# The first two terms of three output products taken into the last score steps, and the last denominators inverted as 16 columns, in a fused attention and MLP block

## The chip, the core and the metric

The kernel runs on one core of a Trainium2 chip. The metric is the device time of one execution in microseconds, lower is better. A core has TensorE (matmuls), VectorE, ScalarE and GpSimd, which run their own instruction queues and wait for each other by semaphores, and DMA queues that are fed here by SyncE. Results of matmuls land in PSUM, which has eight banks of 128 partitions x 512 fp32 values.

## The reference

One transformer block with a modulated layernorm ahead of each half. S = 2048 rows, D = 512, 32 heads of 16 columns, F = 1792, fp32.

```python
x = A_x
mod = (_silu(c) @ w_mod).reshape(c.shape[0], 6, 1, -1)
sa, ca, ga, sb, cb, gb = (mod[:, 0], mod[:, 1], mod[:, 2], mod[:, 3], mod[:, 4], mod[:, 5])
h = _layernorm(x, axis=-1) * (1 + ca) + sa
x = x + ga * _A_ref(h, A_wqkv, A_wo)
h = _layernorm(x, axis=-1) * (1 + cb) + sb
x = x + gb * _B_ref(h, B_w1, B_b1, B_w2)
return x
```

`_A_ref` is softmax attention over all rows, `softmax(q k^T * 16^-0.5) v`, followed by the output product with `wo`. `_B_ref` is `mish(h @ w1 + b1) @ w2`, with mish(a) = a * tanh(softplus(a)).

## The kernel before

**Precision.** A product of fp32 operands is made of three matmuls in the fast fp32 format: each operand is split into a high and a low part, and high x high, high x low and low x high are summed in PSUM. So one output product over D = 512 has four blocks k of 128 rows, with three terms each: 12 matmuls of 128 x 128 by 128 x 512.

**Steps.** Attention goes over 4 blocks of 512 queries (`qb`) and 8 groups of 4 heads (`g`); `n = 8 qb + g` counts the 32 pairs, and each has 16 steps, one for 128 keys. T = 512 steps in all. In a step the kernel emits:

- the scores of four heads for 128 keys, L531: matmuls whose contraction is 64 rows, so that each uses one half of the array's rows (a row group); ScalarE takes the exponential of each (L534);
- the maxima of the scores 20 steps ahead (L482, L484), as long as there is a later pair: `PRO` is 20, so the last 20 steps have no maxima;
- a part of the MLP of the query block before, taken from a queue of units (`units`, `next_part`). A unit of 12 matmuls is spread over two pairs of steps, six slots each. `mm_half` (L135) issues each slot twice, in the even step with the upper 64 rows of the contraction and in the odd one with the lower 64, both times in the row group that the step's own scores do not use;
- `pv` (L549), the product of probabilities and values for the step t - 2: eight passes, which use all rows.

In a step without maxima, f MLP halves stand in the list `beside` and the step's four scores in `mine`, spread between them. If f is under 4, o = (4 - f) // 2 of the scores move to the other row group. Halves of one bank in different row groups must not run at once, so the first half of a step waits for an exponential (`cur["after"]`), that of the score emitted behind the last half of the step before; `next_part` drops this wait when it starts a new unit.

**PSUM.** Six banks are a ring (`ring`, `NRING`) for scores, maxima and some tail products; two more have the tags `ms` (MLP units) and `acc` (probabilities times values). `free_banks` drops dependencies between ring instructions that touch different banks.

**End of a head group.** `evac` copies the 128 x 512 sums of a head group to `ot`; row 16 of each head's 32 rows holds the denominators. They are inverted by way of DMAs, and `od` times the inverse, split in high and low, becomes `o_hl`, the input of the output product (k = g // 2). For the very last group there is no time for DMAs: `evac_last` takes one matmul with a constant matrix `pick` (two passes, L610), which puts the head rows into partitions 64 to 127 and each head's denominator, 16 times, into partitions 0 to 63, and inverts those 64 x 512 values (L611).

**Tail.** After the last step `tail` computes the output product and the MLP of the last 512 rows, with nothing else to run beside. The output product is emitted as the terms k = 0, 1, 2 of four products of 128 rows (`wo_mms`, L1002), with `evac_last` after the first of them, and then k = 3 of all four, each followed by its addition to x (L1014) and a layernorm. Held-back MLP units of the query block before (`held`, L129) and the transposes (L1035) follow, and the last MLP. The weights `wos` and the first `w1s` are loaded at step T - 15 (`tail_loads`) into `ka` tiles that hold no keys any more (L970), the rows of x by the tail itself (L993).

All loads and stores are issued by SyncE from one queue, in the order of the hooks (`at`, `run_hooks`: two half-steps per step).

Of the kernel before, what the change touches and what calls it, by code (L numbers as in the profile page):

```python
# [8 lines left out]
F32 = mybir.dt.float32  # L9
# [9 lines left out]
def adaln_block(ctx: ExitStack, tc: tile.TileContext, x, wqkv, wo, w1, b1, w2, c, w_mod, out):  # L19
    nc = tc.nc  # L20
    P = 128
    S, D = x.shape[1], x.shape[2]
    F = w1.shape[1]
    H = 32
    DH = D // H
    DK = D // P
    FT = F // P
    TB = 512
# [4 lines left out]
    T = 16 * NIT  # L33
# [3 lines left out]
    VROW = NKC * 4 * VW + 16  # L37
    LEAD = 4
    PRO = 16 + LEAD
# [6 lines left out]
    x = x[0]  # L46
# [11 lines left out]
    woscr = dram.tile([DK, P, 2, D], F32, name="woscr")  # L58
# [4 lines left out]
    ident = cst.tile([P, P], F32, name="ident")  # L63
# [20 lines left out]
    gates = [cst.tile([P, D], F32, name=f"gate{i}") for i in range(2)]  # L84
# [61 lines left out]
    NRING = 6  # L146
    ring_t = ps.tile([P, NRING, TB], F32, name="ring")
    ring_at = [0]

    def ring(w=1):  # L150
        if w == 2 and ring_at[0] % 2:
            ring_at[0] += 1
        b = ring_at[0] % NRING
        ring_at[0] += w
        return ring_t[:, b, :] if w == 1 else ring_t[:, b:b + 2, :]
# [41 lines left out]
    def at(h, f):  # L197

        hooks.setdefault(h, []).append(f)
# [4 lines left out]
    ka = [kq.tile([P, S], F32R, name=f"ka{i}") for i in range(2)]  # L204
# [116 lines left out]
    with ExitStack() as es:  # L321
# [68 lines left out]
        for i in range(2):  # L390
            pr.append(ring())
            for k in range(DK):
                nc.tensor.matmul(pr[i][32 * k:32 * k + 32, :], sil[:, k:k + 1].to_broadcast([P, 32]), wma[i][:, k, :],
                                 start=True, stop=True)
# [34 lines left out]
        for tb in range(NB):  # L429
# [5 lines left out]
            for kind in (1, 0) if tb == 0 else (1,):  # L435
                fin = qk_unit(kind, 0, tb, "ring")
# [26 lines left out]
    ap = ctx.enter_context(tc.tile_pool(name="ap", bufs=1, reuse_waits="tile"))  # L463
# [90 lines left out]
    o_hl = {}  # L554
    st, mst = {}, {}
# [42 lines left out]
    def make_pick():  # L598
# [3 lines left out]
        for i, src in enumerate((cols[:, :, DH:DH + 1].to_broadcast([P, 4, DH]), cols[:, :, :DH])):  # L602
            nc.gpsimd.tensor_copy(pick[:, i, :].rearrange("p (h w) -> p h w", w=DH), src)

    def evac_last(dn):

        ot, od, rb = mst["last"]
        oh, ol = o_hl[NB - 1]
        r = slice(64, P)
        nc.tensor.matmul(dn, mst["pick"].rearrange("p a w -> p (a w)"), ot, start=True, stop=True)  # L610
        nc.vector.reciprocal(rb[r], dn[:64, :])  # L611
        nc.vector.tensor_mul(od[r], dn[r, :], rb[r])
        hi_copy("v", oh[r, DK - 1, :], od[r])
        lo_sub("v", ol[r, DK - 1, :], od[r], oh[r, DK - 1, :])

# [348 lines left out]
    last = NB - 1  # L964
    _, w1s, w2s, wos = state[last]

    def half_tile(t, j, scr):

        w = t[:, j * 2 * D:(j + 1) * 2 * D]
        nc.sync.dma_start(w.bitcast(F32), scr.rearrange("p v m -> p (v m)"))  # L970
        return w.rearrange("p (v m) -> p v m", v=2)

    def w1_tail(f):
        i, j = divmod(f % 8, 2)
        return load_w1(f) if i == 1 else half_tile(ka[(1, 0, 2, 3)[i]], j, w1scr[f])

    def tail_loads():
        for k in range(DK):
            wos[k] = half_tile(ka[(4, 0)[k // 2]], k % 2, woscr[k])
        for f in range(2):  # L980
            w1s[f] = w1_tail(f)

    def tail():

        oh, ol = o_hl[last]
        mp = mst["p"]
        y, xn = [], []
        for v in (y, xn):
            for i in range(4):
                v.append(ap.tile([P, D], F32, tag=f"p{i}", name="y", bufs=3 + i % 2))  # L990
        for i in range(4):
            r = 4 * last + i
            nc.sync.dma_start(y[i], x[r * P:(r + 1) * P, :])  # L993
        for f in range(4, 8):
            w1s[f] = w1_tail(f)
        accs4 = [bank("ms"), bank("acc")] + [None, None]

        def wo_mms(i, ks):
            s = slice(i * P, (i + 1) * P)
            seq = [(l, r, k) for l, r in ((oh, 0), (oh, 1), (ol, 0)) for k in ks]  # L1000
            for j, (l, r, k) in enumerate(seq):
                nc.tensor.matmul(accs4[i], l[:, k, s], wos[k][:, r, :], start=(k == 0 and j == 0),  # L1002
                                 stop=(k == 3 and j == 2))

        norms = []
        wo_mms(0, (0, 1, 2))
        evac_last(ring())
        wo_mms(1, (0, 1, 2))
        for i in (2, 3):
            accs4[i] = bank("ring")  # L1010
            wo_mms(i, (0, 1, 2))
        for i in range(4):
            wo_mms(i, (3,))
            nc.vector.tensor_add(y[i], accs4[i], y[i])  # L1014
# [73 lines left out]
        for u in range(FT + LAG):  # L1088
# [14 lines left out]
            f = u - LAG  # L1103
            if f >= 0:
                a_h, a_l = act.pop(f)
                w = w2s.pop(f)
                for i in range(4):
                    s = slice(i * P, (i + 1) * P)
                    for j, (l, r) in enumerate(((a_h, 0), (a_h, 1), (a_l, 0))):
                        nc.tensor.matmul(po[i // 2][:, i % 2, :], l[:, s], w[:, r, :], start=(f == 0 and j == 0),  # L1110
                                         stop=(f == FT - 1 and j == 2))
                    if f == FT - 1 and i % 2:
                        for q in (i - 1, i):
                            nc.vector.tensor_add(y[q], po[q // 2][:, q % 2, :], y[q])
                            r = 4 * last + q
# [9 lines left out]
    cur = {"left": [], "fin": None, "part": []}  # L1125
# [7 lines left out]
    def next_part(h):  # L1133

        if not cur["left"] and units and h >= units[0][0]():
            cur["fin"] = units.pop(0)[1]("ms")
            cur["left"] = list(pe_queue)
            cur.pop("after", None)
            pe_queue.clear()
        slots = []  # L1140
        for m in cur["left"]:
            if slots and len(slots[-1]) < 2 and m[0].shape[-1] <= TB // 2:
                slots[-1].append(m)
            else:
                slots.append([m])
        n = len(slots)
        k = n if n <= 8 else (n + 1) // 2
        cur["part"], cur["left"] = slots[:k], [m for l in slots[k:] for m in l]
# [24 lines left out]
    def step(t):  # L1173
        second = t % 2
        n, u = t // 16, t % 16 // 2
        tm = t + PRO
        run_hooks(2 * t)
        if t < 0:

            for i in range(2):  # L1180
                if tm < 16:
                    kb, jq = divmod(2 * tm + i, 8)
                else:
                    jq, kb = tm % 16 // 2, 2 * second + i
                max_pair(tm // 16, jq, kb)
            if second and tm % 16 == 15:
                neg_max(tm // 16)
            run_hooks(2 * t + 1)
            for f in ats.pop(t, []):
                f()  # L1190
            whole_units(2 * t + 1, CREDIT)
            do_specials(2 * t + 1)
            return
        s = 0 if second else 1
        own, others = ([score(n, j, v, 2 * u + i) for i in range(2) for j in range(2)] for v in (s, 1 - s))
        if not second and 1 < t < T:
            next_part(2 * t)
        part = list(cur["part"])
        f = len(part)
        if t >= T:  # L1200
            if t == T:
                cur["tag"] = "acc"
            run_hooks(2 * t + 1)
            pv(t - 2)
            whole_units(2 * t + 1, 8)
            do_specials(2 * t + 1)
            return
        if tm < T:
            o = max(0, (8 - f) // 2)
            mo, alone = maxima(tm // 16, tm % 16 // 2, s, o)  # L1210

            mine = [x for p in zip(mo, own) for x in p] + own[len(mo):]
        else:
            o = max(0, (4 - f) // 2)
            mine = own[o:] if second else own[:4 - o]
            alone = others[4 - o:] if second else others[:o]

            m = len(mine)
            if f > m:
                mine = [mine[(i * m) // f] if (i + 1) * m // f > i * m // f else None for i in range(f)]  # L1220
        beside = part + alone

        def emit(product):
            e = product()
            if e is not None and cur.pop("want", None):
                cur["after"] = e

        mid = False
        for i in range(max(len(mine), len(beside))):
            if i == len(mine) // 2:  # L1230
                run_hooks(2 * t + 1)

            if not f and tm < T and i == (2 if mst.get("norming") else 3):
                pv(t - 2)
                mid = True
            if i < f:
                last = i + 1 == f
                if i < len(mine) and mine[i] and not last:
                    emit(mine[i])
                for m in beside[i]:  # L1240
                    mm_half(m, second, cur.pop("after", None))
                if last:
                    cur["want"] = True
                    if i < len(mine):
                        emit(mine[i])
                    if second and not cur["left"]:
                        cur["fin"](2 * t + 2)
                        cur["fin"] = None
            else:
                for x in (*mine[i:i + 1], *beside[i:i + 1]):  # L1250
                    emit(x)
        if tm < T and tm % 16 == 15:
            neg_max(tm // 16)
        do_specials(2 * t + 1)
        if not mid:
            pv(t - 2)
        for f in ats.pop(t, []):
            f()
# [89 lines left out]
    for qb in range(NB - 1):  # L1348
        t0 = 32 * G * (qb + 1) + 16
        at(161, lambda qb=qb, t0=t0: block(qb, t0))  # L1350
    at(2 * T - 200, make_pick)
    at(2 * T - 30, tail_loads)
    for pp in range(2, NR):
        for b in (48, 112):
# [10 lines left out]
    t = T + 2  # L1365
# [32 lines left out]
```

## Time and profile before

| | |
|---|---|
| runs before (3) | median 1705.93 us, 1703.87 to 1709.53 |
| span of the profiled execution | 1705.4 us |
| TensorE busy | 1678.7 us, 98% |
| VectorE busy | 1439.9 us, 84% |
| ScalarE busy | 1364.9 us, 80% |
| GpSimd busy | 808.0 us, 47% |
| last L549 of the score stage begins | 1599.74 us |
| tail's first matmul | 1602.45 us |

The profile is one execution, and its span is measured from the first to the last instruction; a run's time is measured around it. In its rows a group stands as line, engine, operation, output<-inputs, tile sizes and a count; the timeline has start and duration in us ahead of it, and in brackets how long the engine had been idle and which instruction released it. PE is a matmul, PEld its weight load, DVE is VectorE, ACT ScalarE, POOL GpSimd, SPq SyncE's queue. The duration of a matmul is from its start until its result is in PSUM; matmuls are pipelined, and what one costs TensorE is the distance to the start of the next.

### The profile page before, as it was taken

How to read it: one execution, taken by the hardware profiler on the slowest of the kernel's cores; microseconds unless marked ns; L12 is line 12 of the kernel's file. 1: busy time of each engine (PE TensorE's matmuls, PEld its weight loads, DVE VectorE, ACT ScalarE, POOL GpSimd, SP SyncE). 2: the span in 40 equal slices, each digit the busy share in tenths (PEclk: the TensorE clock that was granted, in tenths of full speed). 3: DMA queues.
4: the chain of work that ended last, by engine and by line, in shares of the span. 5: the costliest groups of instructions: out<-in, count | busy, mean ns of one | idle time of the engine just before them, and what ended most of it. 6: DMA issues, size and time to landing. Idle time of an engine off the chain costs nothing.

```text
span 1705.4 us, 33628 instructions
## 1 busy us (share of the span) xinstructions
PE 1678.7 (98%) x12372; PEld 956.8 (56%) x12372; DVE 1439.9 (84%) x2368; ACT 1364.9 (80%) x2613; POOL 808.0 (47%) x829
## 2 busy tenths in 40 slices
PE   7999999999999999999999999999999999999999
PEld 5755655555445555555555555555555455554587
DVE  6888888888889998888889998888889988883377
ACT  6257777777778988888888988888888988888574
POOL 5155224665413464655423564555323655555442
PEclk9999999999999999999999999999999999999999
DMA  7677467777773342534355433424354433524261
GB/s 253 183 235 210 116 161 213 242 228 221 237 209 100 98 105 78 137 79 123 84 154 145 119 75 94 139 74 125 85 144 124 128 93 78 150 59 156 85 228 63
DMA packets 113997, 240.08 MB, mean 141 GB/s; under 512 B 24048, under 2 KB 49648, under 8 KB 107784
## 3 DMA queue, kind: packets, MB, share of 16 engines
q1 hardware_dynamic: 113832, 237.92, 48.8%
q8 instruction: 98, 1.61, 0.4%
q14 instruction: 67, 0.55, 0.1%
HBM read 179.95 MB, written 51.44 MB: 136 GB/s over the span
## 4 chain that ended last, share of the span: by engine, by line
PE 90%; DMA 4%; DVE 3%; ACT 1%; SPq 1%; issue 1%; POOL 0%; ACTq 0%; DVEq 0%; POOLq 0%
PE bk L549 28%; PE ring L482 21%; PE ring L531 19%; PE bk L135 12%; PE bk L129 3%; PE ring L1110 2%; PE ring L129 2%; DVE mx L484 1%; DMA qa<-mt 1%; DMA ka<-kscr 1%; DMA xt<-in_A_x 1%; PE ring L496 1%; ACT pr L534 1%; DMA w<-woscr 1%; DMA w<-w1scr 0%
## 5 line engine op out<-in xcount | busy, mean ns | idle before, releaser
L484 DVE TENSOR_REDUCE mx<-ring 128x1 f32<-128x512 f32 x1968 | 1222.1, 682 | 157.7 <-PE ring L482 134.1
L534 ACT ACTIVATE pr<-ring 128x512 f32<-128x512 f32 x2048 | 1085.6, 601 | 215.5 <-PE bk L135 131.2
L482 PE MATMUL ring<-ka,qa 64*128 64x512 f32 x1968 | 834.2, 427 | 5.2 <-DMA od<-ot 2.7
L531 PE MATMUL ring<-qa,ka 64*128 64x512 f32 x2048 | 724.5, 397 | 4.2 <-ACT pr L534 2.2
L482 PEld LDWEIGHTS ring<-ka,qa 64*128 64x128 f32 x1968 | 359.6, 184 | 405.8 <-DVE mx L484 341.2
L549 PE MATMUL bk<-pr,vg 128*32 128x512 f32 x4096 | 545.1, 604 | 0.0
L531 PEld LDWEIGHTS ring<-qa,ka 64*128 64x128 f32 x2048 | 373.8, 184 | 81.3 <-ACT pr L534 23.6
L135 PE MATMUL bk<-h,w 64*128 64x512 f32 (+1 forms) x1080 | 280.2, 393 | 0.1
L135 PE MATMUL bk<-w,a_h 64*128 64x512 f32 x632 | 213.0, 417 | 0.3 <-ACT pr L534 0.2
L135 PEld LDWEIGHTS bk<-h,w 64*128 64x128 f32 x1080 | 178.2, 184 | 12.3 <-ACT pr L534 3.7
L549 PEld LDWEIGHTS bk<-pr,vg 128*32 128x32 f32 x4096 | 80.7, 108 | 132.0 <-issue 124.6
L135 PE MATMUL bk<-w,a_l 64*128 64x512 f32 x316 | 124.0, 392 | 0.0
L135 PEld LDWEIGHTS bk<-w,a_h 64*128 64x128 f32 x632 | 104.7, 184 | 16.6 <-ACT pr L534 8.3
L899 POOL TENSOR_TENSOR y<-yd,y 128x512 f32<-128x512 f32 x44 | 56.8, 1292 | 89.5 <-ACT yd L898 84.4
L750 POOL TENSOR_TENSOR qq<-qq,rr 128x512 f32<-128x512 f32 x42 | 54.3, 1292 | 89.8 <-ACT rr L744 89.6
L734 POOL TENSOR_SCALAR qq<-ee 128x512 f32<-128x512 f32 x25 | 15.5, 619 | 168.0 <-ACT ee L728 168.0
L736 POOL TENSOR_TENSOR hb<-hb,ee 128x512 f32<-128x512 f32 x42 | 54.1, 1288 | 82.5 <-DVE ee L732 80.5
L135 PE MATMUL bk<-w,o_hl 64*128 64x512 f32 x288 | 79.6, 408 | 0.0
L98 POOL TENSOR_TENSOR a_l<-hb,a_h 128x512 fp32r<-128x512 f32 x53 | 72.0, 1359 | 4.4
L135 PEld LDWEIGHTS bk<-w,a_l 64*128 64x128 f32 x316 | 58.3, 184 | 3.9
L135 PE MATMUL bk<-h_h,wl 64*128 64x512 f32 x168 | 56.7, 418 | 0.0
L752 POOL TENSOR_TENSOR rr<-rr,qq 128x512 f32<-128x512 f32 x42 | 54.2, 1291 | 3.5
(189 smaller groups left out, 1844.2 us busy)
## 6 DMA issues: line engine op xcount, KB each, us to landing
ka<-kscr SPq DMA_DIRECT2D x124, 384.0 KB
w<-w2scr SPq DMA_DIRECT2D x56, 512.0 KB
w<-w1scr SPq DMA_DIRECT2D x46, 512.0 KB
vg<-vscr SPq DMA_DIRECT2D x32, 552.0 KB
qa<-qscr SPq DMA_DIRECT2D x124, 100.0 KB
kscr<-qh SPq DMA_DIRECT2D x16, 512.0 KB
qscr<-qh SPq DMA_DIRECT2D x32, 256.0 KB
hl<-in_B_w SPq DMA_DIRECT2D x28, 256.0 KB
```

What stands on the lines that cost most here:

```text
L98: (nc.gpsimd if eng == "p" else nc.vector).tensor_sub(lo, src, hi.bitcast(F32))
L129: nc.tensor.matmul(acc, l, r, start=start, stop=stop)
L135: i = nc.tensor.matmul(acc, l[64 * g:64 * g + 64], r[64 * g:64 * g + 64], start=start and not g, stop=bool(stop and g))
L482: nc.tensor.matmul(pm, qt[64 * s:64 * s + 64, qs * P:(qs + 1) * P], kt[64 * s:64 * s + 64, kb * TB:(kb + 1) * TB], start=True, stop=True)
L484: nc.vector.tensor_reduce(out=mxs[n][:, s, 4 * j + qs, kb:kb + 1], in_=pm, op=ALU.max, axis=AX.X)
L531: nc.tensor.matmul(p_, kt[64 * s:64 * s + 64, kc * P:(kc + 1) * P], qt[64 * s:64 * s + 64, :], start=True, stop=True)
L534: e = nc.scalar.activation(pr, p_, AF.Exp, scale=SCALE)
L549: nc.tensor.matmul(accs[n][32 * h:32 * h + 32, :], vgs[n][:, o:o + 32], pts.pop((t, h)), start=(kc == 0), stop=(kc == 15))
L736: (nc.vector if tail else nc.gpsimd).tensor_mul(hb, hb, ee)
L750: nc.gpsimd.tensor_mul(qq, qq, rr)
L752: nc.gpsimd.tensor_mul(rr, rr, qq)
L899: nc.gpsimd.tensor_add(y[i], yd, y[i])
```

## The change

Two edits. First, the terms k = 0 and 1 of the output products i = 0, 1, 2 of the last query block (6 of 12 matmuls each, 18 in all) are no longer emitted in the tail but, as halves, in the last 18 steps, in bank 5 of the ring, which the ring leaves out from step T - 20 until the tail; after each product VectorE adds it to the rows of x. For this the weights of k = 0, 1 and three blocks of x are loaded earlier. Second, the denominators of the last head group are gathered as 128 x 16 values by four matmuls with four columns of the identity, inverted, copied out to 16 equal columns each, and brought back to rows by four matmuls with the identity; the product with `pick` stays, for the head rows, which ScalarE copies to `od`.

```diff
+    kept = []
     def ring(w=1):
         if w == 2 and ring_at[0] % 2:
             ring_at[0] += 1
+        if kept and ring_at[0] % NRING == NRING - 1:
+            ring_at[0] += 1
...
+    def sums_last(cs):
+        ot = mst["last"][0]
+        for q in range(4):
+            nc.tensor.matmul(cs[:, 4 * q:4 * q + 4], ot[:, q * P:(q + 1) * P], ident[:, DH::32], start=True, stop=True)
+        rc = ap.tile([P, 16], F32, tag="rc", name="rc", bufs=2)
+        nc.vector.reciprocal(rc, cs[:, :16])
+        wide = ap.tile([P, TB], F32, tag="p0", name="wide", bufs=3)[:, :256].rearrange("p (q h d) -> p q h d", q=4, h=4)
+        mst["rc"] = wide
+        nc.vector.tensor_copy(wide, rc.rearrange("p (q h) -> p q h", h=4)[:, :, :, None].to_broadcast([P, 4, 4, DH]))
+
+    def heads_last(dn):
+        ot, od, _ = mst["last"]
+        nc.tensor.matmul(dn, mst["pick"].rearrange("p a w -> p (a w)"), ot, start=True, stop=True)
+        nc.scalar.copy(od[64:], dn[64:, :])
+
     def evac_last(dn):
-        ot, od, rb = mst["last"]
+        od, rc = mst["last"][1], mst["rc"]
         oh, ol = o_hl[NB - 1]
         r = slice(64, P)
-        nc.tensor.matmul(dn, mst["pick"].rearrange("p a w -> p (a w)"), ot, start=True, stop=True)
-        nc.vector.reciprocal(rb[r], dn[:64, :])
-        nc.vector.tensor_mul(od[r], dn[r, :], rb[r])
+        for q in range(4):
+            nc.tensor.matmul(dn[64:, q * P:(q + 1) * P], rc[:, q].rearrange("p h w -> p (h w)"), ident, start=True, stop=True)
+        nc.vector.tensor_mul(od[r], dn[r, :], od[r])
         hi_copy("v", oh[r, DK - 1, :], od[r])
         lo_sub("v", ol[r, DK - 1, :], od[r], oh[r, DK - 1, :])
...
+    FIRST = 3
+    first_of = {"left": [], "fin": None, "part": [], "next": 0}
+    ys = {}
+    def load_wos(ks):
+        for k in ks:
+            wos[k] = half_tile(ka[(4, 0)[k // 2]], k % 2, woscr[k])
+    def load_ys(js):
+        for i in js:
+            ys[i] = gates[i] if i < 2 else ap.tile([P, VROW], F32, tag="vg", name="vg", bufs=2)[:, :D]
+            r = 4 * last + i
+            nc.sync.dma_start(ys[i], x[r * P:(r + 1) * P, :])
     def tail_loads():
-        for k in range(DK):
-            wos[k] = half_tile(ka[(4, 0)[k // 2]], k % 2, woscr[k])
+        load_wos((2, 3))
         for f in range(2):
             w1s[f] = w1_tail(f)
+    def first_part(h):
+        u = first_of
+        if not u["left"] and u["next"] < FIRST:
+            i = u["next"]
+            u["next"] += 1
+            oh, ol = o_hl[last]
+            acc = ring_t[:, NRING - 1, :]
+            s = slice(i * P, (i + 1) * P)
+            seq = [(l[:, k, s], wos[k][:, v, :]) for l, v in ((oh, 0), (oh, 1), (ol, 0)) for k in range(2)]
+            u["left"] = [[(acc, l, r, j == 0, j == len(seq) - 1)] for j, (l, r) in enumerate(seq)]
+            u["fin"] = lambda: nc.vector.tensor_add(ys[i], acc, ys[i])
+        u["part"], u["left"] = u["left"][:2], u["left"][2:]
...
-                v.append(ap.tile([P, D], F32, tag=f"p{i}", name="y", bufs=3 + i % 2))
-        for i in range(4):
+                v.append(ys[i] if v is y and i < FIRST else ap.tile([P, D], F32, tag=f"p{i}", name="y", bufs=3 + i % 2))
+        for i in range(FIRST, 4):
...
-        wo_mms(0, (0, 1, 2))
+        kept.clear()
+        wo_mms(0, (2,))
+        sums_last(ring())
+        heads_last(ring())
         evac_last(ring())
-        wo_mms(1, (0, 1, 2))
+        wo_mms(1, (2,))
         for i in (2, 3):
             accs4[i] = bank("ring")
-            wo_mms(i, (0, 1, 2))
+            wo_mms(i, (2,) if i < FIRST else (0, 1, 2))
...
-            cur.pop("after", None)
+            if not first_of["left"]:
+                cur.pop("after", None)
...
         part = list(cur["part"])
+        if not second:
+            first_of["part"] = []
+            if t == T - PRO:
+                kept.append(NRING - 1)
+            elif T - PRO < t < T:
+                first_part(2 * t)
+        g = len(part)
+        part += first_of["part"]
         f = len(part)
...
-                    if second and not cur["left"]:
+                    if second and g and not cur["left"]:
                         cur["fin"](2 * t + 2)
                         cur["fin"] = None
+                    if second and first_of["part"] and not first_of["left"]:
+                        first_of["fin"]()
...
+    at(2 * (T - 29), lambda: load_wos((0, 1)))
+    at(2 * (T - 28), lambda: load_ys((0, 1)))
+    at(2 * (T - 12), lambda: load_ys((2,)))
     at(2 * T - 30, tail_loads)
```

## What is predicted

> **What bounds the kernel now.** I read the page first, for the engine that sets the time.
>
> ```profile
> span 1705.4 us, 33628 instructions
> PE 1678.7 (98%) x12372; PEld 956.8 (56%) x12372; DVE 1439.9 (84%) x2368; ACT 1364.9 (80%) x2613; POOL 808.0 (47%) x829
> PE 90%; DMA 4%; DVE 3%; ACT 1%; SPq 1%; issue 1%; POOL 0%; ACTq 0%; DVEq 0%; POOLq 0%
> ```
>
> TensorE is busy for 98% of the span and holds 90% of the chain that ended last. So the question is where matmul time is added and where it is taken away, and whether it is on that chain at both places. The change touches two places: the last steps of the score stage, and the first microseconds of the tail. I cut the span there. The 18 steps that will carry new matmuls (T-18 to T-1) run from the start of one probability-times-value group (L549, one per step) at 1551.96 to that of the 18th one after it, at 1599.74.
>
> ```profile
> core 0: us, PE busy (x) PEld busy (x) DVE busy (x) ACT busy (x) POOL busy (x), PEclk, DMA share, GB/s
> 1551.96:1599.74 47.78, 47.40 (x326) 21.69 (x325) 5.12 (x8) 42.28 (x83) 26.79 (x26) 1.00 0.26 95
> ...
> 1602.45:1611.78 9.33, 9.33 (x42) 7.26 (x39) 5.16 (x4) 0.59 (x1) 0.00 (x0) 1.00 0.96 335
> ```
>
> These 18 steps take 47.78 us, 2.654 us each. TensorE is busy for 47.40 of them, ScalarE for 42.28, and the granted clock is full. Two engines are near their limit, so the order inside one step decides. Here is one step from the timeline of TensorE, between two L549 groups; columns are start, duration, engine, line.
>
> ```profile
> 1589.17 1.07 PE L549 MATMUL bk<-pr,vg 128*32 128x512 f32 x8
> 1590.24 0.50 PE L135 MATMUL bk<-w,a_h 64*128 64x512 f32 x1
> 1590.24 0.49 PE L531 MATMUL ring<-qa,ka 64*128 64x512 f32 x1
> 1590.58 0.39 PE L135 MATMUL bk<-w,a_h 64*128 64x512 f32 x1
> 1590.58 0.39 PE L531 MATMUL ring<-qa,ka 64*128 64x512 f32 x1
> 1590.81 0.39 PE L135 MATMUL bk<-w,a_l 64*128 64x512 f32 x1
> 1590.82 0.39 PE L531 MATMUL ring<-qa,ka 64*128 64x512 f32 x1
> 1591.04 0.39 PE L135 MATMUL bk<-w,a_h 64*128 64x512 f32 x1
> 1591.04 0.39 PE L531 MATMUL ring<-qa,ka 64*128 64x512 f32 x1
> 1591.27 0.39 PE L135 MATMUL bk<-w,a_h 64*128 64x512 f32 x1
> 1591.51 0.40 PE L135 MATMUL bk<-w,a_l 64*128 64x512 f32 x1
> 1591.83 1.06 PE L549 MATMUL bk<-pr,vg 128*32 128x512 f32 x8
> ```
>
> A half of an MLP matmul (L135, 64 rows of the array) starts at the same moment as a score (L531, the other 64 rows): these two do run beside each other. But there are six halves and only four scores. After the fourth pair the halves go on alone, one every 0.23 us (1591.04, 1591.27, 1591.51), and L549, which needs all rows, waits for the last. A step is therefore six halves in a row (1590.24 to 1591.83, 1.59 us) and L549 (1.07 us): 2.66 us. The row group of the scores has two free places, that of the halves none. Two more rows: L135 alone over the 18 steps, and ScalarE in the step above.
>
> ```profile
> 1551.96:1599.74 47.78, 29.82 (x109) 18.55 (x108) 1.00 0.26 95
> ...
> 1590.78 2.06 ACT L534 ACTIVATE pr<-ring 128x512 f32<-128x512 f32 x4 [0.59 <-PE ring L531]
> ```
>
> The 108 weight loads of halves (second x) in 18 steps are six each: all steps are of this kind. The second row is ScalarE: four exponentials in 2.06 us, after 0.59 us of waiting for a score. In steps without other work ScalarE waits for TensorE, and not the other way round.
>
> **What the change adds to these steps.** Two rows of the chain of waits, in the tail, give the price of full matmuls and of transposes there.
>
> ```profile
> 1618.90 0.87 PE ring L1035 x8
> ...
> 1687.56 11.80 PE ring L1110 x51
> ```
>
> `first_part` appends two slots to the six, at every even step of the 18, and both steps of the pair issue them as halves: 9 x 2 x 2 = 36 halves. They are 18 matmuls of 512 columns (three products, two k, three terms). A half has 64 rows but the same 512 columns, and its place costs 0.23 us, as the step above shows; the 51 full matmuls in 11.80 us are 0.231 us each, the same. I calculate with 0.232.
>
> `mm_half` puts every half of a step into the row group that the step's own scores do not use. That is the group with no free place. So f goes from 6 to 8, and the step from 2.66 to 2.66 + 2 x 0.232 = 3.12 us. Over 18 steps 36 x 0.232 = 8.35 us. Waiting that is there now could cover some of it; but 18 x 2.66 = 47.9 us stand against 47.78 measured, so these steps hold hardly any, and I allow 0.15 us. I take **+8.2 us**. Bounds: nothing, if the halves found free places; and 18 x (0.34 + 0.232) = 10.3 us, if the change of bank between an MLP half and a new half cost the spacing of the step's first pair (1590.24 to 1590.58).
>
> The Trainium skill, TensorEngine Tiling (Array Packing), Overview, gives up to twice the speed for a contraction of 64 rows, because the tiles of the array work independently. The trace agrees only where the other row group has a matmul (the four pairs above); by that rule in full, 8 + 4 passes would fill six places and the steps would cost nothing, a rival below.
>
> **What else is added to the steps, at no cost.** The rows for it: a copy on VectorE in these steps, and DMA issues on SyncE.
>
> ```profile
> L898 DVE COPY yd<-bk 128x512 f32<-128x512 f32 x3 | 2.1, 692 | 16.2 <-PE bk L135 16.2
> ...
> 1553.95 3.21 SPq L970 DMA_DIRECT2D ka<-woscr  x4
> ...
> 1602.43 1.82 SPq L993 DMA_DIRECT2D y<-in_A_x  x4
> 1604.30 2.01 SPq L970 DMA_DIRECT2D ka<-w1scr  x4
> ```
>
> Three additions of a product into y on VectorE, 0.69 us each like the `yd` copy above, one every six steps; VectorE is busy for 5.12 of 47.78 us. An addition stands behind the unit's own last instruction in VectorE's queue, so the bank of the next unit is released first; the next new half comes over 1.5 us after the addition. If VectorE were full they would cost 2.1 us. The score ring loses one of six banks: a score then waits for the exponential of five scores back, at the latest the third of the step before, which is over by then. Two weight loads move from step T-15 to T-29, and three loads of x from the tail to T-28 and T-12.
>
> Issuing these five takes 2 x 0.8 + 3 x 0.45 = 3.0 us of SyncE's queue, against 47.78 us in which the DMA share is 0.26. They write a ka tile whose last pair ends before step T-32, the two gate tiles that only the weights' preparation read, and the v tile of the head group before the last, read up to T-15: none is still in use, so the queue is held for its 3.0 us at most, no matmul of the next step waits for what stands behind, and the tail's w1 loads go out 1.4 us earlier.
>
> **What the tail loses and gets.** The tail's first part is quoted with its rows, because TensorE has no gap in it, but a chain through VectorE runs beside.
>
> ```profile
> 1602.45 2.36 PE L1002 MATMUL bk<-ka,o_hl 128*128 128x512 f32 x9
> 1602.59 0.59 ACT L563 COPY ot<-bk 128x512 f32<-128x512 f32 x1 [1.77 <-PE bk L549]
> 1604.65 1.02 PE L610 MATMUL ring<-ot,pick 128*128 128x512 f32 x2
> 1605.71 3.35 DVE L611 RECIPROCAL rb<-ring 64x512 f32<-64x512 f32 x1 [5.10 <-PE ring L610]
> 1609.09 0.69 DVE L612 TENSOR_TENSOR od<-ring,rb 64x512 f32<-64x512 f32 x1
> 1609.82 0.42 DVE L93 CAST o_hl<-od 64x512 fp32r<-64x512 f32 x1
> 1610.28 0.69 DVE L98 TENSOR_TENSOR o_hl<-od,o_hl 64x512 fp32r<-64x512 f32 x1
> 1611.78 1.55 PE L1002 MATMUL bk<-ka,o_hl 128*128 128x512 f32 x6
> ```
>
> The 3.35 us reciprocal is over, with what follows, at 1610.97. TensorE comes to the matmuls that need it (k = 3) at 1611.78. So the reciprocal is hidden now, with 0.8 us to spare, and making it short gains nothing by itself. It is a condition of the other edit: with 18 matmuls fewer, TensorE would arrive 4.2 us earlier and wait.
>
> Two rows of the first 200 us have operations like those that are added.
>
> ```profile
> L399 PE MATMUL bk<-sel,row 128*128 128x1 f32 x16 | 1.9, 251 | 0.0
> L584 DVE RECIPROCAL rc<-sm 128x16 f32<-128x16 f32 x1 | 0.2, 240 | 0.0
> ```
>
> Removed: 18 x 0.232 = -4.18 us. Added: sums of four columns, 4 matmuls of two passes each (fp32 takes two, as L610 x2 for one matmul shows); the nearest row is the one-column matmuls at the start (L399). They take 1.9/16 = 0.119 us each although they stream one column: 8 x 0.119 = +0.95. The spreading back is 8 passes of 128 columns, like the transposes (L1035, 0.87 for 8): +0.87. The pick matmul stays (two passes). Waiting: `ot` is written until 1603.18, while three matmuls instead of nine cover only until about 1603.2; then a weight load that cannot be ahead of its matmul, and a change of tiling: +0.2. The 16-column reciprocal (0.24) and a copy of 256 columns (0.4 at most, by the cast of 512) run while the pick matmul does (0.86), so TensorE hardly waits for them. Then multiplication, cast and subtraction (0.69 + 0.42 + 0.69 and gaps, 1.9 us) run beside 15 matmuls (3.5 us). Sum: -4.18 + 0.95 + 0.87 + 0.2 = **-2.2 us**. Bounds: -3.9 if the small passes cost almost nothing, -0.3 if each cost as much as 512 columns (16 x 0.232 = 3.7).
>
> For the sums the Trainium skill, TensorE: Matmul & The Clock Gate, Back-to-back issue gap, counts about 60 cycles for any width from 1 to 64, 25 ns with its floor; an estimate from that page is 0.2 us for 8 passes and a gain of 2.9 in the tail. The measured 0.119 us decides here.
>
> Behind 1611.78 nothing is changed: additions, layernorm, transposes and the MLP follow in the same order, and TensorE stays the bound, so the gain goes through to the end.
>
> **Sum.** 1705.4 + 8.2 - 2.2 = 1711.4 us of span. The median of the runs shown, 1705.93, is 0.5 above the profiled span, so I predict 1711.9 for the median, +0.35%.
>
> **The rivals.**
> *Free places are used (not slower).* The two halves stream in the two places that the scores leave free. The step stays at 2.66, and only the tail's gain is left: 1711.9 - 8.2 = 1703.7. Against it: the free places are in the other row group, and the trace shows halves starting alone at 0.23 us. It decides if the step stays below 2.8 us. 8%.
> *The exponentials become the chain (more slower).* The first half of a step waits for the exponential of the score that was issued after the last half. That score now comes after the eighth. From the step's start: 0.34 + 6 x 0.232 = 1.73, then 0.54 to the exponential (1590.24 to 1590.78) and 0.6 for it: 2.87, below 3.12. But ScalarE has eight MLP operations in these steps, two in each of four rows, of which three stand here.
>
> ```profile
> L534 ACT ACTIVATE pr<-ring 128x512 f32<-128x512 f32 x74 | 38.3, 604 | 5.4 <-PE ring L531 5.0
> L741 ACT ACTIVATE rr<-ee,two 128x512 f32<-128x512 f32 x2 | 1.5, 746 | 0.0
> L725 ACT ACTIVATE ee<-hb,hcap 128x512 f32<-128x512 f32 x2 | 1.5, 744 | 0.0
> ...
> L744 ACT ACTIVATE rr<-rr 128x512 f32<-128x512 f32 x2 | 1.3, 658 | 0.0
> ```
>
> Where one falls between the third and the fourth, the step is 2.87 + 0.74 = 3.61, 0.5 more: with six such steps +3, 1714.9. Against it: they now fall behind the fourth. 9%.
> *The tail gives nothing back.* If the sums, the short reciprocal, the copy and the second pass follow each other with their waits exposed, some 2 us of idle TensorE take the place of what was removed: 1711.9 + 2.2 = 1714.1. For it: four crossings between engines; against it: the pick matmul covers them. 10%.
> *My forecast*: 70%, from 1709.8 (tail at -3.9 and some cover) to 1713.5. The remaining 3% are causes not listed.
>
> **How the numbers follow.** A measurement of this kernel tells a change from none at about 0.3%, 5.1 us, so slower begins at 1711.05. The forecast lies above it, with some four fifths of its chance; with the two slower rivals this gives 0.70 x 0.83 + 0.09 + 0.10 = 0.77 for slower. The rest of the forecast and the first rival are within 0.3%: 0.70 x 0.17 + 0.08 = 0.20. Faster would need the first rival and another 3 us: 0.03. The range 1709.0 to 1714.9 holds the forecast and the two slower rivals, and leaves out the first.
>
> **What would show it.** Right: the timeline shows eight halves in a step and L549 groups 3.05 to 3.15 us apart, 18 steps in about 56 us; the tail's k = 3 matmuls start some 9.3 - 2.2 = 7.1 us after the first tail matmul; the stretch behind has its length unchanged. Wrong: steps below 2.9 us (free places), idle TensorE released by L534 at the steps' starts (exponentials), or idle TensorE between the pick matmul and the second pass (tail). If the steps come out at 2.66, the prediction is wrong in its largest term.

## The result and the profile after

| | before | after |
|---|---|---|
| runs | median 1706.74 us (22 runs, 1702.20 to 1711.67) | median 1711.82 us (22 runs, 1708.49 to 1717.95) |
| ratio to before | | 1.0027, 95% interval 1.0019 to 1.0035 |
| span of the profiled execution | 1705.4 us | 1709.6 us |

The change makes the kernel slower by 0.27%, some 4.6 us by the ratio; the two medians lie 5.1 us apart. That the predicted 1711.9 came within 0.1 us of the median is luck: the predicted difference (+6.0) was 0.9 us larger than that of the medians, and with more runs the median of before moved up by 0.8 us. The page of the changed kernel:

```profile
span 1709.6 us, 33702 instructions
PE 1685.0 (99%) x12406; PEld 961.5 (56%) x12406; DVE 1438.6 (84%) x2372; ACT 1367.6 (80%) x2614; POOL 808.2 (47%) x829
PE 94%; DVE 2%; DMA 2%; ACT 1%; issue 0%; POOL 0%; SPq 0%; ACTq 0%; DVEq 0%; POOLq 0%
```

TensorE got 6.3 us more to do and its share of the chain rose. Busy time by stretch shows where (column 2 is the length, the rest as in the prediction's first view of this kind); the cuts are the same events as in the kernel before: 18 steps, last L553 group (L549 before), tail to the first k = 3 matmul, k = 3, rest.

```profile
1551.07:1605.90 54.83, 54.83 (x361) 28.23 (x361) 6.70 (x11) 44.64 (x83) 26.82 (x26) 1.00 0.20 69
1605.90:1608.61 2.71, 2.71 (x25) 0.68 (x24) 1.00 (x2) 0.72 (x2) 1.27 (x1) 1.00 0.03 13
1608.61:1615.71 7.10, 7.10 (x39) 5.27 (x36) 2.36 (x5) 1.17 (x2) 0.00 (x0) 1.00 0.96 359
1615.71:1618.51 2.80, 2.80 (x14) 2.27 (x13) 1.59 (x4) 0.00 (x0) 0.00 (x0) 1.00 0.06 20
1618.51:1709.60 91.09, 87.09 (x408) 71.89 (x406) 71.33 (x97) 53.98 (x82) 34.70 (x38) 1.00 0.37 136
```

The stretches of the kernel before that were not shown yet:

```profile
1599.74:1602.45 2.71, 2.71 (x25) 0.68 (x25) 0.69 (x1) 1.07 (x3) 1.28 (x1) 1.00 0.00 0
...
1611.78:1614.56 2.78, 2.78 (x13) 2.26 (x12) 1.76 (x4) 0.00 (x0) 0.10 (x1) 1.00 0.27 109
1614.56:1705.40 90.84, 86.87 (x407) 71.70 (x405) 71.27 (x97) 53.95 (x82) 34.60 (x38) 0.99 0.36 136
```

The 18 steps went from 47.78 to 54.83 (+7.05), the tail up to k = 3 from 9.33 to 7.10 (-2.23), everything between and behind by 0.0, 0.0 and +0.25. The sum of the two places is +4.8 us, 0.28% of the time, which is the measured ratio. The stretch ahead of the 18 steps was 0.89 us shorter in this execution; the same point came anywhere from 1549.78 to 1555.62 us in the executions shown below, so single spans are no measure of half a microsecond, while the length of a stretch is.

One step of the changed kernel, TensorE alone, from the timeline:

```profile
1602.85 1.06 PE L553 MATMUL bk<-pr,vg 128*32 128x512 f32 x8
1603.85 0.49 PE L135 MATMUL bk<-w,a_h 64*128 64x512 f32 x1
1603.85 0.50 PE L535 MATMUL ring<-qa,ka 64*128 64x512 f32 x1
1604.18 0.40 PE L135 MATMUL bk<-w,a_h 64*128 64x512 f32 x1
...
1604.65 0.62 PE L135 MATMUL bk<-w,a_h 64*128 64x512 f32 x2
1604.89 0.50 PE L535 MATMUL ring<-qa,ka 64*128 64x512 f32 x1
1605.11 0.39 PE L135 MATMUL bk<-w,a_l 64*128 64x512 f32 x1
1605.35 0.62 PE L135 MATMUL ring<-ka,o_hl 64*128 64x512 f32 x2
1605.90 1.49 PE L553 MATMUL bk<-pr,vg 128*32 128x512 f32 x12
```

Six MLP halves, then the two new ones (inputs `ka,o_hl`) with no score beside them, then L553. The row group of the halves has eight passes, the other four. The step takes 3.05 us (3.046 in the mean of the 18), where 3.12 were predicted. The difference is at its start: the first half follows L553 by 1.00 us (1602.85 to 1603.85), where the step shown before had 1.07.

The tail, from the timeline:

```profile
1608.61 0.96 PE L1050 MATMUL bk<-ka,o_hl 128*128 128x512 f32 x3
1608.75 0.59 ACT L567 COPY ot<-bk 128x512 f32<-128x512 f32 x1 [2.05 <-PE bk L553]
1609.41 1.04 PE L613 MATMUL ring<-ident,ot 128*128 128x4 f32 x8
1610.30 1.10 PE L623 MATMUL ring<-ot,pick 128*128 128x512 f32 x2
1610.54 0.26 DVE L615 RECIPROCAL rc<-ring 128x16 f32<-128x16 f32 x1 [3.64 <-issue]
1610.83 0.29 DVE L618 COPY wide<-rc 128x256 f32<-128x256 f32 x1
1611.34 1.09 PE L632 MATMUL ring<-ident,wide 128*64 128x128 f32 x8
...
1612.35 0.53 PEld L1050 LDWEIGHTS bk<-ka,o_hl 128*128 128x128 f32 x3 [0.17 <-issue]
```

The reciprocal went from 3.35 to 0.26 us, and the sums and the spreading back take TensorE from 1609.41 to 1610.30 (0.89) and from 1611.34 to the next matmul's weight load at 1612.35 (1.0).

### The profile page after: what moved, and what is told of

Its sections match the earlier page's. It is cut to its first block, busy times and chain, and to the rows that moved or that the text cites. A ratio compares the mean times of both kernels' runs of the same rounds, so it can differ in the third digit from the quotient of the medians.

```text
span 1709.6 us, 33702 instructions
## 1 busy us (share of the span) xinstructions
PE 1685.0 (99%) x12406; PEld 961.5 (56%) x12406; DVE 1438.6 (84%) x2372; ACT 1367.6 (80%) x2614; POOL 808.2 (47%) x829
## 4 chain that ended last, share of the span: by engine, by line
PE 94%; DVE 2%; DMA 2%; ACT 1%; issue 0%; POOL 0%; SPq 0%; ACTq 0%; DVEq 0%; POOLq 0%
PE bk L553 29%; PE ring L486 21%; PE ring L535 21%; PE bk L135 12%; PE bk L129 3%; PE ring L1161 2%; PE ring L129 2%; DVE mx L488 1%; DMA xt<-in_A_x 1%; PE ring L500 1%; ACT pr L538 1%; DMA qa<-mt 1%; PE ring L135 0%; PE ring L864 0%; DVE ee L753 0%; PE ring L515 0%
## 5 line engine op out<-in xcount | busy, mean ns | idle before, releaser
L535 PE MATMUL ring<-qa,ka 64*128 64x512 f32 x2048 | 730.2, 398 | 4.9 <-ACT pr L538 2.1
L553 PE MATMUL bk<-pr,vg 128*32 128x512 f32 x4096 | 545.7, 605 | 0.0
L535 PEld LDWEIGHTS ring<-qa,ka 64*128 64x128 f32 x2048 | 374.1, 184 | 81.8 <-ACT pr L538 23.6
L553 PEld LDWEIGHTS bk<-pr,vg 128*32 128x32 f32 x4096 | 80.8, 108 | 132.2 <-issue 125.1
```

What stands on the lines that cost most here:

```text
L535: nc.tensor.matmul(p_, kt[64 * s:64 * s + 64, kc * P:(kc + 1) * P], qt[64 * s:64 * s + 64, :], start=True, stop=True)
L553: nc.tensor.matmul(accs[n][32 * h:32 * h + 32, :], vgs[n][:, o:o + 32], pts.pop((t, h)), start=(kc == 0), stop=(kc == 15))
```

## The experiments

Two theories stood against each other on the steps. Theory R, from the prediction: TensorE alone needs 2.66 us for a step with six halves, and every added half costs 0.23. Theory L, formed on the result: in the kernel before, the step was closed by a loop through ScalarE, and TensorE alone needs 2.585. This row of the kernel before is the weight load of the first half behind the step that the prediction shows:

```profile
1592.90 0.18 PEld L135 LDWEIGHTS bk<-w,a_h 64*128 64x128 f32 x1 [0.91 <-ACT pr L534]
```

It names an exponential as what released the half. First half and score at 1590.24, first exponential at 1590.78, four of them until 1592.84, next half at 1592.90: 0.54 + 2.06 + 0.06 = 2.66 us, as long as six halves and L549. Both ways round the step came out nearly equal. The bracket does not decide between them, for the changed kernel has almost the same one:

```profile
1601.35 2.22 ACT L538 ACTIVATE pr<-ring 128x512 f32<-128x512 f32 x4 [0.77 <-PE ring L535]
...
1603.85 0.18 PEld L135 LDWEIGHTS bk<-w,a_h 64*128 64x128 f32 x1 [0.84 <-ACT pr L538]
```

There the exponentials end at 1603.57, 0.28 us before the half, and still stand in the bracket. The bracket counts from the last weight load of the group before it, so 0.84 us is its value when nothing is waited for; the wait in the kernel before is only what goes beyond, 0.91 - 0.84 = 0.07 us. What does tell the two apart is a step of the kernel before in which the wait is dropped because a new MLP unit starts:

```profile
1594.49 1.07 PE L549 MATMUL bk<-pr,vg 128*32 128x512 f32 x8
1595.49 0.18 PEld L135 LDWEIGHTS bk<-w,a_h 64*128 64x128 f32 x1 [0.84 <-DVE yd L898]
...
1597.08 0.16 PEld L549 LDWEIGHTS bk<-pr,vg 128*32 128x32 f32 x8 [0.37 <-issue]
```

This step takes 2.59 us, with the same six halves. Five of the 18 are of this kind, each 2.58 or 2.59 us long, and the other 13 take 2.64 to 2.77. So the profile before already spoke for theory L; the next two runs test it.

**One slot in place of two.** For one product, seven halves in 12 steps.

```diff
-    FIRST = 3
+    FIRST = 1
-        u["part"], u["left"] = u["left"][:2], u["left"][2:]
+        u["part"], u["left"] = u["left"][:1], u["left"][1:]
...
-        wo_mms(1, (2,))
+        wo_mms(1, (0, 1, 2))
...
-    at(2 * (T - 28), lambda: load_ys((0, 1)))
-    at(2 * (T - 12), lambda: load_ys((2,)))
+    at(2 * (T - 28), lambda: load_ys((0,)))
```

> One added slot per pair of steps in place of two, for one product: 12 steps with seven halves, the rest with six. Theory L (before, a step of 2.66 us was closed by ScalarE's four exponentials, and TensorE alone needs 2.585): the 12 steps take 2.585 + 0.232 = 2.82 us each. Rival R (as predicted: TensorE alone needs 2.66): 2.66 + 0.232 = 2.89 us each.

The twelve steps, from L553 group to L553 group:

```profile
1555.62:1589.40 33.78, 33.78 (x230) 16.64 (x229) 3.80 (x7) 29.70 (x58) 14.77 (x15) 1.00 0.31 103
```

33.78 / 12 = 2.815 us each, as theory L expects. With six, seven and eight halves the step is 2.654, 2.815 and 3.046 us: the second added half costs its full 0.231, the first only 0.161. (Its one timed run, 1713.67 us, is too few to say anything of the total.)

**ScalarE made shorter, in the kernel before.**

```diff
-            e = nc.scalar.activation(pr, p_, AF.Exp, scale=SCALE)
+            if 16 * n + 15 >= T - 16 and kc % 2 == 0 and j == 0:
+                e = nc.scalar.activation(pr[:, :256], p_[:, :256], AF.Exp, scale=SCALE)
+                nc.vector.tensor_copy(pr[:, 256:], p_[:, 256:])
+            else:
+                e = nc.scalar.activation(pr, p_, AF.Exp, scale=SCALE)
```

> The kernel before, but in the last 16 steps one of the four exponentials of each step is taken on 256 of its 512 columns, and VectorE copies the other 256 as they are (the probabilities of those columns are left out). Theory L (before, the step is closed by ScalarE: half, score, four exponentials, next half): ScalarE's chain is 0.25 us shorter and no longer the longest, TensorE sets the steps, 2.59 us each in place of 2.66. Rival R (as predicted, TensorE alone sets 2.66): the steps stay at 2.65 to 2.66.

Fifteen of the steps by stretch, and two rows of ScalarE's timeline in them (L535 is the exponential of 256 columns):

```profile
1559.65:1598.39 38.74, 38.74 (x271) 18.12 (x270) 10.38 (x22) 31.75 (x68) 23.50 (x22) 1.00 0.20 70
```

```profile
1571.55 0.38 ACT L535 ACTIVATE pr<-ring 128x256 f32<-128x256 f32 x1 [0.78 <-PE ring L531]
1571.84 1.57 ACT L538 ACTIVATE pr<-ring 128x512 f32<-128x512 f32 x3
```

38.74 / 15 = 2.583 us. Nothing on TensorE was changed, and its steps became 0.07 us shorter, as short as the five of the kernel before that did not wait. So 2.583 us is TensorE's own need and the rest was ScalarE's loop: theory L is shown, theory R is not. Over 18 steps the cover is 47.78 - 18 x 2.583 = 1.3 us. The busy times show only 0.4 us of it (47.78 - 47.40), since a matmul counts as busy until its result is in PSUM.

**The ring of five banks, alone.** The kernel before, with these lines of the change:

```diff
+        if kept and ring_at[0] % NRING == NRING - 1:
+            ring_at[0] += 1
...
+        if t == T - PRO:
+            kept.append(NRING - 1)
...
+        kept.clear()
```

> The kernel before with the ring at five banks from step T-20 on, and nothing else. As predicted (no cost): the 18 steps take 47.6 to 48.0 us as before. Rival (the bank costs): scores wait for a bank, steps of 2.7 us or more.

```profile
1551.82:1599.60 47.78, 47.39 (x325) 21.69 (x324) 5.12 (x8) 42.28 (x83) 26.83 (x26) 1.00 0.27 95
```

47.78 us, the same as before: the bank costs nothing. (This kernel and the one ahead of it were timed once each, so only their stretches are read.)

**The added halves in the free row group.** As the changed kernel, but a new half is issued in the row group of the step's scores, ahead of the fourth and the sixth MLP half.

```diff
+    def first_half(m, second):
+        acc, l, r, start, stop = m
+        g = 1 - second
+        nc.tensor.matmul(acc, l[64 * g:64 * g + 64], r[64 * g:64 * g + 64], start=start and not second, stop=bool(stop and second))
...
-        g = len(part)
-        part += first_of["part"]
-        f = len(part)
+        g = f = len(part)
+        more = list(first_of["part"])
...
+                if i in (3, 5) and more:
+                    first_half(more.pop(0)[0], second)
```

> As the changed kernel, but the added halves use the other row group, that of the step's own scores, in the two places that these leave free (behind the second and the third score). Theory A (a place in the row group of the MLP halves is the whole cost): the 18 steps take 47.6 to 48.2 us in place of 54.8, the tail keeps its gain of 2.2, total about 1703.5 to 1704.5, 2 to 3 us below the kernel before. Rival (any added half costs its passage, whatever its rows): 54 to 55 us, total as the changed kernel. Between them: a score is pushed back and the exponentials with it, 2.9 us per step.

The 18 steps and the tail up to k = 3, and then the timeline of one step (L541 is a score, L145 a new half):

```profile
1552.14:1600.22 48.08, 47.70 (x361) 22.25 (x360) 6.41 (x10) 42.30 (x83) 26.91 (x26) 1.00 0.23 78
1602.93:1610.04 7.11, 7.11 (x40) 5.27 (x36) 2.36 (x5) 1.17 (x2) 0.00 (x0) 1.00 0.91 343
```

```profile
1591.16 0.39 PE L135 MATMUL bk<-w,a_l 64*128 64x512 f32 x1
1591.16 0.39 PE L145 MATMUL ring<-ka,o_hl 64*128 64x512 f32 x1
...
1591.63 0.39 PE L135 MATMUL bk<-w,a_h 64*128 64x512 f32 x1
1591.63 0.39 PE L145 MATMUL ring<-ka,o_hl 64*128 64x512 f32 x1
1591.86 0.40 PE L135 MATMUL bk<-w,a_l 64*128 64x512 f32 x1
1591.86 0.39 PE L541 MATMUL ring<-qa,ka 64*128 64x512 f32 x1
```

Each new half now starts together with an MLP half. The steps hold the same 144 halves as in the changed kernel and take 48.08 us in place of 54.83; the tail keeps its 7.1 us. The ratio to the kernel before is 0.9984, 95% interval 0.9975 to 0.9993: the same work is faster than before by 0.16%. The total was 1705.17 us (11 runs) beside 1707.54 for the kernel before on that chip; the 1703.5 to 1704.5 expected were reckoned against 1705.9. So the whole loss of the change is the choice of the row group.

The step's passes on TensorE are not longer here: from the first half (1590.59) to L559 (1592.18) it is 1.59 us, as with six halves alone. The 0.3 us that remain have a likely source, which no run takes out: three steps that begin a new MLP unit while an output product is under way now keep the wait for an exponential, which the kernel before drops there, and take 2.68 to 2.73 us in place of 2.59.

**The 16-column denominators alone.** The kernel before with `sums_last`, `heads_last` and the new `evac_last`, and all terms of the output products in the tail.

```diff
         wo_mms(0, (0, 1, 2))
+        sums_last(ring())
+        heads_last(ring())
         evac_last(ring())
```

> Only the second edit: the 16-column denominators, with all output-product terms still in the tail. Theory A (the reciprocal was hidden before, so the edit only adds passes to TensorE): the stretch from the tail's first matmul to its first k = 3 matmul goes from 9.33 us to about 11.2 (+0.95 for the sums, +0.87 for spreading back), the steps before stay at 2.654 us, total +1.8 us (+0.1%). Rival (the reciprocal's chain still cost something): the stretch stays at 9.3 or falls.

```profile
1549.78:1597.55 47.77, 47.39 (x326) 21.70 (x325) 5.12 (x8) 42.28 (x83) 26.82 (x26) 1.00 0.27 95
1600.26:1611.46 11.20, 11.20 (x58) 8.73 (x54) 2.36 (x5) 1.17 (x2) 0.00 (x0) 1.00 0.85 305
```

11.20 against 9.33 us: the edit alone costs 1.87 us, since the long reciprocal was hidden. VectorE's busy time in the stretch fell from 5.16 to 2.36 us, and nothing came of it. The total agrees: ratio 1.0020, interval 1.0009 to 1.0031.

**The moved terms alone.** The changed kernel with the old `evac_last`.

```diff
-        sums_last(ring())
-        heads_last(ring())
         evac_last(ring())
```

> Only the first edit: the first two terms moved into the steps, with the old reciprocal of 64x512 in the tail. Steps as in the changed kernel, 3.05 us. Theory A (the second edit costs more than the wait that it removes): TensorE waits about 1.2 us for the reciprocal's chain (3.35 + 0.69 + 0.42 us after the pick matmul) while 15 matmuls run, so the first k = 3 matmul comes 6.4 to 6.9 us after the tail's first, against 7.10 in the changed kernel; total 0.2 to 0.6 us below the changed kernel. Rival (the second edit is a condition of the first): 8 us or more, 1 us or more above it.

```profile
1553.94:1608.77 54.83, 54.83 (x362) 28.25 (x361) 6.70 (x11) 44.63 (x83) 26.78 (x26) 1.00 0.21 69
1611.48:1618.03 6.55, 5.39 (x24) 3.60 (x20) 4.51 (x4) 0.59 (x1) 0.00 (x0) 1.00 0.96 345
```

TensorE now idles 1.2 us in the stretch (6.55 - 5.39) for the reciprocal's chain, and still reaches k = 3 after 6.55 us, 0.55 earlier than with the second edit. Some of that goes again behind it, where the third k = 3 matmul waits for the low part (2.97 us to the next unit against 2.80), so what is left is about 0.4 us. The second edit is no condition of the first: it removes a wait of 1.2 us and puts 1.7 us of work on TensorE in its place (7.10 us busy against 5.39). The total (ratio 1.0031, interval 1.0020 to 1.0041) can't tell this kernel from the changed one.

**Both findings together.** The free row group with the old `evac_last`.

> The added halves in the free row group, and the first edit alone: the old reciprocal of 64x512 in the tail. If both findings add up: steps of 2.67 us as with the free row group, the first k = 3 matmul 6.55 us after the tail's first, total some 2.5 us (0.15%) or a little more below the kernel before, 0.4 us below the free row group with the 16-column denominators, which a total can't resolve. Rival: the two interfere, steps of 2.7 us or a tail of 7 us or more.

```profile
1554.87:1602.98 48.11, 47.70 (x361) 22.24 (x360) 6.41 (x10) 42.31 (x83) 26.85 (x26) 1.00 0.24 78
1605.69:1612.24 6.55, 5.39 (x24) 3.61 (x20) 4.50 (x4) 0.59 (x1) 0.00 (x0) 1.00 0.94 350
```

Both stretches are as short as they were singly, and the ratio is 0.9984, interval 0.9972 to 0.9996: also faster than before, and, as expected, not to be told by its total from the kernel with the free row group alone.

## Why the prediction was right, and where not

- **The place of the added halves.** It said that the halves go into the row group that has no free place and cost their passes. Shown: eight halves in a row in the timeline, the free row group taking the same halves for 0.3 us in all, and 0.231 us for the second half of a step.
- **The cover in the steps** is the term that was mis-sized. The prediction set 18 x 2.66 against 47.78, found "hardly any" waiting, allowed 0.15 us, and wrote that ScalarE waits for TensorE "and not the other way round". It was 1.3 us: 2.66 was taken from a step that itself waited for an exponential, so setting it against the measured 47.78 could not show the wait. The 1.07 us taken for L549 was 1.00 and 0.07 of waiting. 36 x 0.232 = 8.35, less 1.3, is 7.05, as measured; +8.2 was predicted. The steps of 3.046 us thus came out just under the 3.05 to 3.15 that the prediction named as its sign.
- **The tail** came out at -2.23 us against -2.2. The parts: the sums 0.89 (0.95 predicted), the spreading back 1.0 (0.87), which leaves 0.06 for waits and change of tiling (0.2), if the 18 removed matmuls are worth the 4.18 reckoned. That a short reciprocal gains nothing by itself was right: alone, the second edit costs 1.87 us. That it is "a condition of the other edit" was wrong: without it TensorE waits 1.2 us and is still earlier.
- **The costs set to nothing** (ring bank, additions on VectorE, moved loads): the bank is shown by itself at 0.00 us. The additions and loads were not taken out one by one, but the 18 steps leave hardly any room for them: 18 x 2.583 + 8.35 = 54.84 us against 54.83 measured.
- **The rivals.** Free places that are used by themselves: no, but they can be used by an edit, and the steps then take the 48 us of that rival. The exponentials as the chain: no; with eight halves the exponentials end about 0.2 to 0.3 us before the half that has to follow them, the half comes 0.99 or 1.00 us behind L553 in every one of the 18 steps, and the 0.07 us that it waited before are gone. A tail that gives nothing back: no.

## What to carry to other kernels

When matmuls of half height run side by side in two row groups, count the passes of each group in a step: the longer list is the step, and an added pass is cheap only in the shorter one: here 0.23 us for each half in the longer list, and 0.3 us for all 36 in the shorter. When two chains through a step are equally long to 0.1 us, an engine named in a bracket does not tell which one closes the loop, since the last to release is named even where it was done in time. Compare steps that have the wait with steps that don't, or shorten one engine alone to find the other's own time; the difference, here 0.07 us a step, is what added work gets for nothing. A slow instruction that is hidden is worth shortening only if the passes added on the bound engine cost less than the wait that would show: here 1.7 us against 1.2.

## What was not expected of the hardware

In these traces matmuls in different row groups do not start in the order of the queue. In the kernel before, a step's order is half, score, half, score, half, half, score, half, half, score; by the rows shown in the prediction the third score starts at 1590.82 with the third half, and the fourth score at 1591.04 with the fourth half, although it stands behind the sixth, at 1591.51, in the queue. The fourth score runs 0.42 to 0.46 us ahead of that half in all 18 steps, and in the changed kernel, where it stands behind eight halves, 0.68 to 0.70 us.

The lead brings the exponential nothing, for a score is reported done only after the halves that were queued before it. The trace keeps the moments at which TensorE raises the semaphore of a score. In the step of the prediction those of the third and fourth score are at 1591.46 and 1591.93, 0.02 us behind the ends of the fourth half (1591.43) and the sixth (1591.90), though by their own rows the two scores end at 1591.20 and 1591.44. All 18 steps of both kernels have it so, to 0.03 us. In the changed kernel the last exponential can be seen to start so late:

```profile
1601.85 0.49 PE L535 MATMUL ring<-qa,ka 64*128 64x512 f32 x1
...
1602.54 0.38 PE L135 MATMUL ring<-ka,o_hl 64*128 64x512 f32 x1
...
1602.97 0.60 ACT L538 ACTIVATE pr<-ring 128x512 f32<-128x512 f32 x1
```

The fourth score ends at 1602.34, the second new half at 1602.92, and the score's exponential begins at 1602.97, 0.65 us after the one before it (1602.32); in the kernel before four take 2.06 us, so they follow each other there by some 0.49 us. The ends of matmuls are modelled in the profile, the semaphores are recorded. No run was made on how far such a lead can go.
